# Two lightweight-convolution channel layouts for the first product of an MLP: three 64-row chunks with copies between partition halves, or one 128-row chunk and one 64-row chunk held twice

## The chip, the cores and the metric

The kernel runs on one core of a Trainium2 chip. The metric is the device time of one execution in microseconds; smaller is better. The engines have short names throughout: PE is the matrix engine (PEld its weight loads), DVE the vector engine, ACT the scalar engine, POOL the general one, SP the engine that here only issues DMAs.

## What is computed

The input x is 8 sequences of 4096 tokens with 192 channels. A causal convolution of 7 taps runs along the tokens; each of 8 groups of 24 channels has its own taps, a softmax over a small weight array. Its result goes through two products with an activation between them, all in 32-bit floats:

```python
idx = np.arange(S)[:, None] + np.arange(K)[None, :]
x_unf = x_pad[:, idx, :].reshape(B, S, K, H, group)
out = np.einsum('hk,bskhg->bshg', w, x_unf)          # 8 x 4096 x 192, K = 7, H = 8
...
h = x @ w_in                                         # 32768 x 192 times 192 x 2048
g = h * (1.0 / (1.0 + np.exp(-1.702 * h)))
return (g @ w_out).astype(np.float32)                # 2048 x 192
```

## The kernel before

**Steps.** The work is cut into 32 steps ("big") of 1024 tokens: 512 tokens of one sequence (index n = 0) and the same 512 of another (n = 1), each in two halves of 256 (index o). The tiles hold channels, or hidden features, on the partitions and tokens along the free dimension. The first step also rounds the weights and is written out by itself (`first_step`); the others are a call of `hidden` and a call of `second`.

**Layout of x.** The 192 channels are three chunks (c) of 64. Partitions 0-63 hold the tokens of o = 0, partitions 64-127 those of o = 1. `load_x` (line 126) brings x in with 8 DMAs in runs of 160 channels, `transpose_x` (145) turns 32x32 blocks on DVE, and the convolution adds seven scaled copies (`tap`, `add_taps`: on ACT, POOL, DVE and by DMAs that add). The result is `own`.

**Three multiplications.** A 32-bit product is made of three faster ones of rounded parts. `split_high` (167, ACT), `split_low` (170, DVE) and `split_both` (173, DVE) make the parts xh, xl and xd of `own`. Each needs all tokens on both partition halves, since half h of the partitions works on hidden features of its own: `cross` (178) copies each half's blocks to the other half, two DMAs on SP for each part and step.

**hidden** (245) makes the 2048 x 1024 hidden values in 16 units. A unit (j, n) is two blocks of 128 features, one per partition half, by the 512 tokens of one n, in two PSUM slots. A unit's work on PE is three passes of six matmuls of 64 rows x 512 columns, in pairs that run side by side on the two row halves of the array:

```python
upper(slot, j, n)     # wh with xh, then wl with xl (line 212, matmul in line 218)
scale(slot, engines)  # both slots times UP, in place, on ACT ("a") or DVE ("v") (line 232)
lower(slot, q, n)     # ring weights with xd, added to the scaled slots (line 223, matmul in line 227)
gelu(slot, j, n)      # ACT writes g (line 236)
```

In turn i of the loop come `upper` and `scale` of unit i, then `lower` and `gelu` of unit i-1, then `extra(i)`: transposes of a later x, parts of the convolution, and from turn 10 on sums of blocks of g for the second product (EARLY_G, DVE). Four pairs of slots take turns. The weights of `lower` come from DRAM through a ring of three buffers, each serving two units, so six units ahead; the loads are issued on SP behind the stores of the last step and the loads of x.

**second** (657 and after) makes the output with a scheme that needs fewer products than the plain one but many sums. g has four rows (r) of four blocks (j = 2n + o), each of four feature blocks: `block(r, j)`, named as a spot with number 5 + 4r + j. Unit (j, n) fills features 2j and 2j + 1 for one n. The order of everything is written out by hand in PLAN: "main" and "side" name products (32-column matmuls, four side by side, line 557), "go" issues one group of four, "sum" is a DVE sum of spots (line 620), "acc" a DMA that adds (line 625), "seed" a copy on ACT (671), "join" a sum of results, "tap" the next piece of a later convolution (513), "high", "low", "both" the splits and crossings of the next step's x, "next" the `upper` of the next step's unit 0. PLAN begins

```python
("side", 13, 16, "k0"), ("main", 1, 5, "p2", 1), ("go", 1), ("high",), ("go", 3),
("sum", 14, 14, "-", 18), ("low",), ("main", 16, 10, "p3", 0), ("go", 4), ("both",),
("main", 0, 14, "p0", 1), ("go", 1), ...
```

The engines take their instructions in this order, each its own.

Of the kernel before, what the change touches and what calls it, by code (L numbers as in the profile page):

```python
# [16 lines left out]
def kernel(  # L17
# [26 lines left out]
    NU = 2  # L44
    NV = 2
    NJ = T // Q + 1
    XT = NJ * Q
    XW = D - Q
    n3 = NC * Q
    assert B % 2 == 0 and NC == 3 and D == NC * R and HD == 3 * Q and S % TOK == 0  # L50
    assert F == 2 * NU * 2 * NV * P and PAD <= Q
# [26 lines left out]
    PAIRS = [(0, 0), (1, 1), (1, 0), (0, 1)]  # L78
    NG = 4
    assert len(PAIRS) * 4 == NF == NG * NG  # L80
# [35 lines left out]

    xt = consts.tile([P, NC, 2, XT], F32)
    own = consts.tile([P, 2 * NC, T], F32)
    xh, xl, xd = (consts.tile([P, 4 * NC, T], F32R, name=f"x{i}") for i in "hld")
    OVER = 2 * NC  # L120

    def xin_of(big):
        flat = flat_room if big == 2 else flat_g(NG - 1)
        return flat[:, 0 : 2 * NJ * XW].rearrange("p (n j d) -> p n j d", n=2, j=NJ)

    def load_x(big, ns=range(2)):

        p, c = divmod(big, CHUNKS)
        xin = xin_of(big)
        if c == 0 and 0 in ns:  # L130
            (nc.gpsimd if big else vec).memset(xin[0:R, :, 0, :], 0.0)
        for n in ns:
            for o in range(2):
                j = 1 if c == 0 and o == 0 else 0
                t = c * TOK + o * T + (j - 1) * Q
                for v in range(2):
                    q0 = o * R + v * Q
                    nc.sync.dma_start(
                        out=xin[q0 : q0 + Q, n, j:NJ, :],
                        in_=x_v[n, p, t : t + (NJ - j) * Q, v * Q : v * Q + XW].rearrange(  # L140
                            "(j i) d -> i j d", i=Q
                        ),
                    )

    def transpose_x(big, c, n=None):
        ns = slice(0, 2) if n is None else slice(n, n + 1)
        vec.transpose(
            xt[:, c, ns, :].rearrange("p n (j t) -> p (n j) t", t=Q),
            xin_of(big)[:, ns, :, :].rearrange("p n j d -> p (n j) d")[:, :, c * R : c * R + Q],
        )  # L150

    def conv_src(c, k, ns=slice(0, 2)):
        return xt[:, c, ns, Q - PAD + k : Q - PAD + k + T]

    def own_of(c, ns=slice(0, 2)):
        return own[:, 2 * c + ns.start : 2 * c + ns.stop, :]

    def conv(c, k, ns=slice(0, 2), times=vec.tensor_scalar_mul):
        src, dst, tap = conv_src(c, k, ns), own_of(c, ns), cw[:, c, k : k + 1]
        if k == 0:  # L160
            times(dst, src, tap)
        else:
            vec.scalar_tensor_tensor(
                out=dst, in0=src, scalar=tap, in1=dst, op0=ALU.mult, op1=ALU.add
            )
# [16 lines left out]
    OWN_ALL, OVER_ALL = slice(0, OVER), slice(OVER, 2 * OVER)  # L182


    wh, wl = (consts.tile([P, 2 * NU, NV, NC, P], F32R, name=f"w{i}") for i in "hl")
    RING = 3
    ring = consts.tile([P, RING, NC, P], F32R)
    N_W = NV * len(PAIRS)
    wd_dram = dram.tile([N_W, P, NC * P], F32)

    def piece_of(j):

        pi, v = j % len(PAIRS), j // len(PAIRS)
        m, u = PAIRS[pi]
        return 2 * u + m, v

    def ring_slot(q):
        return ring[:, q % RING]

    def load_ring(q):  # L200
        if q < N_W * N_BIG:
            nc.sync.dma_start(out=wide(ring_slot(q)).rearrange("p k f -> p (k f)"), in_=wd_dram[q % N_W])

    NX = 2 * N_W

    def operand(t, h, b):
        both = t[halves[h], b : b + OVER + 1 : OVER, :]
        return both if h == 0 else both[:, ::-1, :]

    KS = (1, 2, 0)  # L210

    def upper(slot, j, n):

        i, v = piece_of(j)
        for w, t in ((wh, xh), (wl, xl)):
            for k in KS:
                for h in range(2):
                    nc.tensor.matmul(  # L218
                        slot[h], w[halves[h], i, v, k, :], operand(t, h, 2 * k + n),
                        start=w is wh and k == KS[0], stop=False, skip_group_check=True,  # L220
                    )

    def lower(slot, q, n):

        for k in KS:
            for h in range(2):
                nc.tensor.matmul(  # L227
                    slot[h], ring_slot(q)[halves[h], k, :], operand(xd, h, 2 * k + n),
                    start=False, stop=k == KS[-1], skip_group_check=True,
                )  # L230

    def scale(slot, engines):
        for h in range(2):
            (act.mul if engines[h] == "a" else vec.tensor_scalar_mul)(slot[h], slot[h], UP)  # L234

    def gelu(slot, j, n):
        r = 2 * (j % len(PAIRS) + j // len(PAIRS) * len(PAIRS))
        for h in range(2):
            act.activation(  # L239
                g[:, r // NG, n, :, r % NG + h, :],  # L240
                slot[h].rearrange("p (o t) -> p o t", o=2),
                AF.Gelu_apprx_sigmoid,
            )
# [17 lines left out]
    def load_later(q):  # L261
        if q >= N_W:
            load_ring(q)
# [42 lines left out]
    def end_forms():  # L306
# [6 lines left out]
    PART = NC * P  # L313
    PIECE = CW * D
    assert PIECE == 2 * PART
    raw = [flat_g(2)[:, 2 * PART * i : 2 * PART * (i + 1)] for i in range(5)]
    raw += [osbs[:, 2 * PART * i : 2 * PART * (i + 1)] for i in range(2)]
    flat_own = own.rearrange("p b t -> p (b t)")
    raw += [flat_own[:, 2 * T : 2 * T + 2 * PART]]
    raw_out = [flat_room[:, 2 * PIECE * i : 2 * PIECE * (i + 1)] for i in range(3)] + [osbs[:, 0 : 2 * PIECE]]  # L320
    assert 10 * PART <= 4 * BLK and 6 * PIECE <= 5 * BLK
    words_in = [flat_form[:, 2 * PART * i : 2 * PART * (i + 1)] for i in range(4)]
    words_out = [flat_form[:, 8 * PART + 2 * PIECE * i : 8 * PART + 2 * PIECE * (i + 1)] for i in range(2)]
    assert 8 * PART + 4 * PIECE <= FORMS * NG * HD
    diag = flat_room[:, 4 * PIECE : 4 * PIECE + 2 * K * R].rearrange("p (c k q) -> p c k q", c=2, k=K)
    all_sel = osbs[:, 2 * PIECE : 2 * PIECE + NC * P].rearrange("i (c q) -> i c q", c=NC)
    sel = all_sel[0:H]
    ident = osbs[:, 2 * PIECE + NC * P :]
    assert 2 * PIECE + (NC + 1) * P == 4 * TOK
    fold = flat_own[:, 6 * T - R : 6 * T]  # L330
    assert 2 * PART + R <= 4 * T
# [10 lines left out]
    load_x(0, (0,))  # L342

    w_in_v = moe_w_in.bitcast(U32).rearrange(
        "(k q) (m u h v f) -> u m h v q k f", q=R, m=2, u=NU, h=2, v=NV
    )
    w_out_v = moe_w_out.bitcast(U32).rearrange("(c p) d -> p c d", p=P)

    def load_w_in(j):
        i, v = piece_of(j)  # L350
        for h in range(2):
            nc.sync.dma_start(
                out=raw[j][halves[h], :].bitcast(U32).rearrange("p (k f) -> p k f", k=NC),
                in_=w_in_v[i // 2, i % 2, h, v],
            )
# [13 lines left out]
    for c in range(NC):  # L369
        part = sel[:, c, :].rearrange("i (h q) -> i h q", h=2)  # L370
        for sign in (1, -1):
# [5 lines left out]
                base=R * c if sign == 1 else group - 1 - R * c,  # L377
                pattern=[[0, 2], [sign, R]],
                channel_multiplier=-sign * group,
            )  # L380
    nc.gpsimd.tensor_add(fold, ident[:, 0:R], ident[:, R:P])
# [12 lines left out]
    def in_part(j):  # L394
        return raw[j], words_in[j % 4]
# [35 lines left out]
    def round_w_in(j):  # L431
# [5 lines left out]
        i, v = piece_of(j)  # L437
        flat = [t[:, i, v].rearrange("p k f -> p (k f)") for t in (wh, wl)]
        low = ring_slot(j).rearrange("p k f -> p (k f)")
# [3 lines left out]
        vec.scalar_tensor_tensor(  # L443
            out=low, in0=rest, scalar=C, in1=wide(flat[0]), op0=ALU.mult, op1=ALU.subtract
        )
        nc.sync.dma_start(out=wd_dram[j], in_=wide(low))

    def round_w_out(i):
        piece = out_piece(i)
        join(piece)  # L450
        pi = PAIRS.index(divmod(i, NU))
        dsts = []
        for m in range(2):
            for v in range(2):
                for h in range(2):
                    dsts.append(
                        (
# [463 lines left out]
```

## Time and profile before

| | |
|---|---|
| median of 3 runs | 2508.43 us (2508.32 to 2519.02) |
| the profiled execution, its own time | 2508.66 us |
| its span, first to last instruction | 2506.8 us |
| busy: PE, DVE, ACT, POOL | 2288.4, 1813.8, 1587.6, 715.4 us |
| granted PE clock, mean over the span | 0.978 |
| first step (hidden from 24.58, second from 91.38) | until 144.53 us |
| second step | until 245.28 us |
| the 29 like steps | until 2428.68 us |
| last step | until the end |

Busy times of different engines lie beside each other, so they don't add up to the span. A row of the profile names the engine, the line of the kernel, the operation, what is written and read (out<-in), the shapes and the count; rows of waits name who waited for whom. In a timeline the first number is the start in us from the beginning of the span and the second the length; a bracket gives the idle time before it and what ended it.

### The profile page before, as it was taken

How to read it: one execution, taken by the hardware profiler on the slowest of the kernel's cores; microseconds unless marked ns; L12 is line 12 of the kernel's file. 1: busy time of each engine (PE TensorE's matmuls, PEld its weight loads, DVE VectorE, ACT ScalarE, POOL GpSimd, SP SyncE). 2: the span in 40 equal slices, each digit the busy share in tenths (PEclk: the TensorE clock that was granted, in tenths of full speed). 3: DMA queues.
4: the chain of work that ended last, by engine and by line, in shares of the span. 5: the costliest groups of instructions: out<-in, count | busy, mean ns of one | idle time of the engine just before them, and what ended most of it. 6: DMA issues, size and time to landing. Idle time of an engine off the chain costs nothing. (4 is left out here: it accounts for less than half of the span.)

```text
span 2506.8 us, 68873 instructions
## 1 busy us (share of the span) xinstructions
PE 2288.4 (91%) x29078; PEld 1579.1 (63%) x29078; DVE 1813.8 (72%) x2598; ACT 1587.6 (63%) x3131; POOL 715.4 (29%) x719
## 2 busy tenths in 40 slices
PE   5769999999999999999999999999999999999998
PEld 4436666666666666666666666666666666666665
DVE  4738777768777678777768777768777768777677
ACT  5636666666666666666666666666666666666643
POOL 0022323332333331333331333332333331323300
PEclk7889999999999999999999999999999999999999
DMA  7377767877766887667887777887666887667753
GB/s 185 76 140 148 153 143 143 172 162 145 150 145 141 167 175 148 147 144 144 173 168 145 150 145 145 174 168 145 147 144 141 174 171 144 145 143 144 146 119 72
DMA packets 302820, 371.69 MB, mean 148 GB/s; under 512 B 120624, under 2 KB 237104, under 8 KB 302512
## 3 DMA queue, kind: packets, MB, share of 16 engines
q0 software_dynamic: 63216, 162.49, 36.2%
q1 hardware_dynamic: 234768, 202.04, 34.2%
q8 instruction: 229, 3.75, 0.6%
q10 hardware_dynamic: 4528, 2.76, 0.5%
q14 instruction: 79, 0.65, 0.1%
HBM read 102.50 MB, written 26.74 MB: 52 GB/s over the span
## 5 line engine op out<-in xcount | busy, mean ns | idle before, releaser
L557 PE MATMUL slot<-g,w_form 128*32 128x256 f32 x8928 | 930.0, 383 | 7.0 <-DVE room L620 4.2
L239 ACT ACTIVATE g<-slot 128x512 f32<-128x512 f32 x1024 | 551.9, 597 | 275.2 <-PE slot L227 246.7
L227 PE MATMUL slot<-xd,ring 64*128 64x512 f32 x3072 | 561.1, 405 | 136.7 <-DVE slot L234 74.5
L234 DVE TENSOR_SCALAR slot<-slot 128x512 f32<-128x512 f32 x651 | 432.0, 694 | 332.3 <-PE slot L218 328.7
L557 PEld LDWEIGHTS slot<-g,w_form 128*32 128x32 f32 x8928 | 478.2, 111 | 161.1 <-DVE room L620 13.5
L557 PE MATMUL slot<-g,w_out_s 128*32 128x256 f32 (+1 forms) x6336 | 532.1, 404 | 38.9 <-DVE g L620 29.1
L218 PE MATMUL slot<-xh,wh 64*128 64x512 f32 x3072 | 513.3, 393 | 21.9 <-ACT wh L440 17.1
L620 DVE TENSOR_TENSOR g<-g 128x1024 f32<-128x1024 f32 x403 | 483.4, 1218 | 61.7 <-DMA g<-room 41.3
L227 PEld LDWEIGHTS slot<-xd,ring 64*128 64x128 f32 x3072 | 359.9, 186 | 242.6 <-DVE slot L234 134.9
L218 PE MATMUL slot<-xl,wl 64*128 64x512 f32 x3072 | 507.7, 389 | 4.5 <-DMA xl<-xl 3.4
L668 ACT COPY room<-slot 32x256 f32<-32x256 f32 x651 | 237.4, 365 | 306.2 <-PE slot L557 300.2
L557 PEld LDWEIGHTS slot<-g,w_out_s 128*32 128x32 f32 x6336 | 262.1, 112 | 266.0 <-issue 51.2
L218 PEld LDWEIGHTS slot<-xh,wh 64*128 64x128 f32 x3072 | 357.2, 185 | 83.6 <-ACT wh L440 20.8
L218 PEld LDWEIGHTS slot<-xl,wl 64*128 64x128 f32 x3072 | 360.7, 185 | 55.0 <-issue 4.8
L513 ACT ACTIVATE g<-xt,cw 128x512 f32<-128x512 f32 x406 | 288.1, 723 | 132.8 <-POOL own L530 72.6
L625 POOL DMA_DIRECT2D g<-g x124 | 128.5, 1036 | 564.9 <-PE slot L557 544.4
L234 ACT ACTIVATE slot<-slot 128x512 f32<-128x512 f32 x373 | 210.0, 579 | 113.4 <-PE slot L218 113.4
L557 PE MATMUL slot<-osbs,w_form 128*32 128x256 f32 x2232 | 226.3, 379 | 0.5 <-issue 0.4
L530 POOL TENSOR_TENSOR own<-own,g 128x512 f32<-128x512 f32 x174 | 220.0, 1284 | 4.5
L557 PE MATMUL slot<-room,w_form 128*32 128x256 f32 x2232 | 171.4, 379 | 0.0
L625 POOL DMA_DIRECT2D g<-osbs x31 | 27.1, 874 | 415.4 <-ACT g L239 415.4
L557 PEld LDWEIGHTS slot<-osbs,w_form 128*32 128x32 f32 x2232 | 116.2, 110 | 43.1 <-issue 1.3
(102 smaller groups left out, 1846.9 us busy)
## 6 DMA issues: line engine op xcount, KB each, us to landing
g<-g POOLq DMA_DIRECT2D x124, 512.0 KB, 13.6
ring<-wd_dram SPq DMA_DIRECT2D x251, 192.0 KB, 2.4
g<-in_x_dram SPq DMA_DIRECT2D x232, 180.0 KB, 4.1
xh<-xh SPq DMA_DIRECT2D x62, 384.0 KB, 3.7
xl<-xl SPq DMA_DIRECT2D x62, 384.0 KB, 6.9
xd<-xd SPq DMA_DIRECT2D x62, 384.0 KB, 12.1
out_dram<-osbs SPq DMA_DIRECT2D x186, 128.0 KB, 4.3
g<-osbs POOLq DMA_DIRECT2D x31, 512.0 KB, 5.0
```

The source lines that it names most:

```text
L218: nc.tensor.matmul(slot[h], w[halves[h], i, v, k, :], operand(t, h, 2 * k + n), start=w is wh and k == KS[0], stop=False, skip_group_check ...
L227: nc.tensor.matmul(slot[h], ring_slot(q)[halves[h], k, :], operand(xd, h, 2 * k + n), start=False, stop=k == KS[-1], skip_group_check=True,)
L234: (act.mul if engines[h] == "a" else vec.tensor_scalar_mul)(slot[h], slot[h], UP)
L239: act.activation(g[:, r // NG, n, :, r % NG + h, :], slot[h].rearrange("p (o t) -> p o t", o=2), AF.Gelu_apprx_sigmoid,)
L513: act.mul(home, conv_src(c, k), cw[:, c, k : k + 1])
L530: eng.tensor_add(dst, dst, home)
L557: nc.tensor.matmul(dst, w, t, start=first, stop=last, skip_group_check=True)
L620: (vec.tensor_add if op == "+" else vec.tensor_sub)(v(dst), v(a), v(b))
L625: nc.gpsimd.dma_start(out=spot(dst), in_=spot(a), accum_op=ALU.add)
L668: act.copy(to, d)
```

## The change

The channels are laid out in another way. Channels 0-127 lie on all 128 partitions, for every token of n = 0 (a = 0) and of n = 1 (a = 1). Channels 128-191 lie on both halves, o = 0 on partitions 0-63 and o = 1 on 64-127 (a = 2), and their weights are held twice, once for each half. So each half needs only its own tokens, and `cross` goes. x is loaded in runs of 32 channels with 16 DMAs a step.

A unit is now one block of 128 features by all 1024 tokens: a slot per o, with n = 0 and 1 side by side in it. A pass is two matmuls of 128 rows, one per slot, and a pair of 64 rows, one per slot; from pass to pass their order alternates (`phase`). `lower` and `gelu` of a unit come two turns after its `upper` instead of one, between the two passes of `upper`; those of the last unit (`end`) have moved into PLAN, behind the fourth group. The ring has six buffers, one unit each. The engines of `scale` are dealt out anew. In the first step the weights are rounded in pieces a third larger, two of the operations go from DVE to POOL, and the first convolution is made with 128-row matmuls.

```diff
+    def load_x(big, parts=(0, 2, 1)):
+        ...
+        for a in parts:
+            if a < 2:
+                ...
+                for q in range(4):
+                    load(one[q * Q : (q + 1) * Q, a], a, c * TOK - Q, q * Q, int(c == 0))
+            else:
+                ...
+                for n in range(2):
+                    for q in range(4):
+                        o, v = divmod(q, 2)
+                        load(two[q * Q : (q + 1) * Q, n], n, c * TOK + o * T - Q, P + v * Q, int(c == 0 and o == 0))
...
-    def cross(t, to, of, eng=nc.sync):
-        for o in range(2):
-            eng.dma_start(out=wide(t[halves[1 - o], to, :]), in_=wide(t[halves[o], of, :]))
...
-    def upper(slot, j, n):
-        i, v = piece_of(j)
-        for w, t in ((wh, xh), (wl, xl)):
-            for k in KS:
-                for h in range(2):
-                    nc.tensor.matmul(
-                        slot[h], w[halves[h], i, v, k, :], operand(t, h, 2 * k + n),
-                        start=w is wh and k == KS[0], stop=False, skip_group_check=True,
-                    )
...
+    def pass_of(slot, w, t, first=False, last=False):
+        phase[0] += 1
+        for step in range(2):
+            if (step + phase[0]) % 2:
+                for o in range(2):
+                    nc.tensor.matmul(
+                        slot[o], w[:, 0, :], t[:, o : o + 3 : 2, :],
+                        start=first and step == 0, stop=last and step == 1, skip_group_check=True,
+                    )
+            else:
+                for o in range(2):
+                    nc.tensor.matmul(
+                        slot[o], w[halves[o], 1, :], t[halves[o], 4:6, :],
+                        start=first and step == 0, stop=last and step == 1, skip_group_check=True,
+                    )
...
+    def end_unit(big, tiles, r):
+        q = big * NF + r
+        lower(tiles[r % 4], q)
+        gelu(tiles[r % 4], r)
+        if q + RING >= NF:
+            load_ring(q + RING)
...
-        for i in range(NX + 1):
-            if i < NX:
-                if i or not begun:
-                    upper(tiles[i % 4], *divmod(i, 2))
-                scale(tiles[i % 4], scales[i])
-            if i:
-                j, n = divmod(i - 1, 2)
-                q = big * N_W + j
-                lower(tiles[(i - 1) % 4], q, n)
-                gelu(tiles[(i - 1) % 4], j, n)
-                if n == 1:
-                    load_later(q + RING)
+        for i in range(NF):
+            if i or not begun:
+                upper_high(tiles[i % 4], i)
+            if i > 1:
+                end_unit(big, tiles, i - 2)
+            if i or not begun:
+                upper_low(tiles[i % 4], i)
+            scale(tiles[i % 4], scales[i])
             extra(i)
+        end_unit(big, tiles, NF - 2)
...
-        vec.tensor_sub(rest, w, wide(flat[0]))
+        nc.gpsimd.tensor_sub(rest, w, wide(flat[0]))
         act.mul(flat[1], rest, C)
-        vec.scalar_tensor_tensor(
-            out=low, in0=rest, scalar=C, in1=wide(flat[0]), op0=ALU.mult, op1=ALU.subtract
-        )
+        nc.gpsimd.tensor_sub(low, wide(flat[1]), wide(flat[0]))
...
-        ("side", 13, 16, "k0"), ("main", 1, 5, "p2", 1), ("go", 1), ("high",), ("go", 3),
+        ("side", 13, 16, "k0"), ("main", 1, 5, "p2", 1), ("go", 1), ("high",), ("go", 3), ("end",),
...
         def high():
             if more:
-                split_high(own, 0, OVER)
-                cross(xh, OVER_ALL, OWN_ALL)
+                split_high(own, 0, 6)
...
-        hidden(0, tiles, ["aa"] * NX, extra, begun=False)
+        hidden(0, tiles, ["av", "vv"] * (NF // 2), extra, begun=False)
+        end_unit(0, tiles, NF - 1)
...
-    SCALES = ["aa", "aa", "va", "vv"] + ["va", "vv"] * 6
+    SCALES = ["av", "av", "av", "vv"] + ["av", "vv"] * 6
```

More of the change, by code (lines that the diff above doesn't have):

```diff
@@ L114, in kept @@
         return spot(KEPT_LATE)[0:n3, i % NG, :]
[L117 to L120, printed above, removed]
+    turned = [consts.tile([P, 2, n * Q], F32, name=f"xt{i}") for i, n in enumerate((NJ2, NJ))]
+    own = consts.tile([P, 6, T], F32)
+    flat_own = own.rearrange("p b t -> p (b t)")
+    xh, xl, xd = (consts.tile([P, 6, T], F32R, name=f"x{i}") for i in "hld")
@@ L160, in conv, with tap_of, own_of @@
+    def tap_of(a, k):
+        return cw[:, a // 2, k : k + 1]
+    def own_of(a):
+        return own[:, 2 * a : 2 * a + 2, :]
+    def conv(a, k, times=vec.tensor_scalar_mul):
+        src, dst, tap = conv_src(a, k), own_of(a), tap_of(a, k)
         if k == 0:
@@ L223, in lower @@
[L223 to L238, printed above, removed]
+    wh, wl = (consts.tile([P, NF, 2, P], F32R, name=f"w{i}") for i in "hl")
@@ L239, in gelu, with upper_high, upper_low, lower @@
+    def upper_high(slot, r):
+        pass_of(slot, wh[:, r], xh, first=True)
+    def upper_low(slot, r):
+        pass_of(slot, wl[:, r], xl)
+    def lower(slot, q):
+        pass_of(slot, ring[:, q % RING], xd, last=True)
+    def scale(slot, engines):
+        for o in range(2):
+            (act.mul if engines[o] == "a" else vec.tensor_scalar_mul)(slot[o], slot[o], UP)
+    def gelu(slot, r):
+        for o in range(2):
             act.activation(
-                g[:, r // NG, n, :, r % NG + h, :],
@@ L341 @@
     act.activation(early, ident[0:H, 0:1], AF.Exp)
[L342 to L346, printed above, removed]
+    load_x(0, (0, 2))
+    w_in_v = moe_w_in.bitcast(U32)
     w_out_v = moe_w_out.bitcast(U32).rearrange("(c p) d -> p c d", p=P)
     def load_w_in(j):
-        i, v = piece_of(j)
-        for h in range(2):
+        dst = raw[j].bitcast(U32).rearrange("p (r k f) -> p r k f", r=2, k=2)
+        cols = slice(4 * P * j, 4 * P * (j + 1))
+        for on, k, rows in ((slice(0, P), 0, 0), (halves[0], 1, P), (halves[1], 1, P)):
+            n = on.stop - on.start
             nc.sync.dma_start(
-                out=raw[j][halves[h], :].bitcast(U32).rearrange("p (k f) -> p k f", k=NC),
-                in_=w_in_v[i // 2, i % 2, h, v],
+                out=dst[on, :, k, :], in_=w_in_v[rows : rows + n, cols].rearrange("q (r f) -> q r f", r=2)
             )
@@ L368 @@
     nc.gpsimd.memset(sel, 1.0)
-    for c in range(NC):
+    for c in range(2):
         part = sel[:, c, :].rearrange("i (h q) -> i h q", h=2)
@@ L478 @@
     warm(5)
-    for c in range(NC):
+    for c in range(2):
         nc.tensor.matmul(
@@ L629, with second @@
     SIDE_HALF = (0, 0, 1, 0, 1, 0, 1)
-    def second(big, bx, bs, by, more, next_first):
+    def second(big, bx, bs, by, more, end, next_first):
         mains, sides = (bs[0], bx[0], by[0]), (bx[1], bs[1], by[1])
@@ L702, in second @@
             join=lambda d, a, op, b: add_up(value, d, a, op, b), turn=out_turn, store=out_store,
-            tap=next_tap, high=high, low=low, both=both, next=next_first,
+            tap=next_tap, end=end, high=high, low=low, both=both, next=next_first,
         )
@@ L707, in second, with first_conv @@
         assert not side and not now["steps"] and count[0] == NC * len(SIDE_HALF)
[L709 removed]
+    def first_conv(a):
         for k in range(K):
[L711 to L727 removed]
@@ L748, in high_first, with first_src @@
-    def high_first(n, i):
-        src, b = first_blocks(n)[i]
-        split_high(src.unsqueeze(1), b, b + 1)
-        cross_first(xh, n, KS[i])
-    def first_step(tiles):
-        one, two = slice(0, 1), slice(1, 2)
-        make_diag()
-        transpose_x(0, 1, 0)
-        transpose_x(0, 2, 0)
+            nc.tensor.matmul(
+                pairs[1][a], diag[:, k, :], conv_src(a, k), start=(k == 0), stop=(k == K - 1), skip_group_check=True
+            )
+    def first_src(a):
+        return (own_of(2) if a == 2 else pairs[1][a].rearrange("p (o t) -> p o t", o=2)), 2 * a, 2 * a + 2
@@ L784, in first_step @@
+        for k in range(2, K):
+            conv(2, k)
+        split_low(*first_src(0))
+        split_both(*first_src(0))
+        split_high(*first_src(2))
+        round_w_in(0)
+        split_high(*first_src(1))
+        split_low(*first_src(2))
+        split_low(*first_src(1))
+        split_both(*first_src(2))
+        split_both(*first_src(1))
         split(in_part(1))
@@ L842, in first_step @@
         turns = second_plain(pb, pa, pc, at)
-        for q in range(N_W, N_W + RING):
-            load_ring(q)
-        upper(pf, 0, 0)
+        upper_high(pf, 0)
+        upper_low(pf, 0)
         for m, n, src in turns:
@@ L888 @@
             ready.extend((c, k) for c in (1, 0, 2) for k in range(K))
-        second(big, pb, pa, pc, more, (lambda: upper(pf, 0, 0)) if more else lambda: None)
+        begin = lambda: (upper_high(pf, 0), upper_low(pf, 0))
+        second(big, pb, pa, pc, more, end, begin if more else lambda: None)
         tiles = [pf, pa, pb, pc]
```

252 lines of the change are left out of this document (89 added, 163 removed).

## The prediction

> **What bounds the kernel now.** First the page's span, then the windows, which cut the run into stages:
>
> ```profile
> span 2506.8 us, 68873 instructions
> ```
>
> ```profile
> 24.58:91.38 66.80, 47.69 (x288) 30.24 (x288) 36.53 (x82) 49.44 (x98) 0.00 (x0) 0.83 0.49 139
> 144.53:210.15 65.62, 39.97 (x289) 31.17 (x289) 40.41 (x54) 28.76 (x53) 6.10 (x7) 0.81 0.47 92
> 245.28:2428.68 2183.40, 2038.76 (x26452) 1417.95 (x26448) 1615.97 (x2259) 1421.32 (x2795) 677.29 (x663) 0.99 0.74 152
> 1148.20:1186.88 38.68, 35.09 (x292) 28.68 (x289) 27.80 (x38) 24.11 (x46) 13.49 (x12) 1.00 0.57 122
> 1186.88:1222.51 35.63, 34.43 (x626) 20.19 (x626) 27.93 (x41) 25.30 (x52) 10.44 (x12) 1.00 0.97 192
> ```
>
> Columns: length, then busy PE, PEld, DVE, ACT, POOL, granted clock, DMA share, GB/s. From 245.28 to 2428.68 the same step runs 29 times, 2183.40 / 29 = 75.3 us each. I work on one of them: a hidden stage H of 38.68 (lines 218 and 227) and an output stage S of 35.63 (line 557). PE is busy 2038.76 of the 2183.40, more than any other: nearly without a gap in S, with gaps in H. The waits of PE say which:
>
> ```profile
> PE slot L227 <- DVE slot L234: 74.5, 66, 6.3
> PE slot L227 <- ACT slot L234: 38.7, 32, 1.6
> PE slot L557 <- DVE g L620: 29.3, 24, 3.2
> ...
> PE slot L218 <- DMA xh<-xh: 4.8, 3, 3.6
> ```
>
> (total, times, longest.) The copies between the halves, which the change removes, cost PE 4.8 us for xh in the whole run, and less for xl, which stands further down, and xd: they are hidden. The gaps of H are the third multiplication (line 227) waiting for the scaling of its slot (line 234).
>
> **The price of PE's work in H.** PE's timeline around the start of H and late in S (start, length, what, count; neighbours of one kind are merged), then its weight loads:
>
> ```profile
> 1147.87 0.39 PE L557 MATMUL slot<-g,w_out_s 128*32 128x256 f32 x3
> 1147.89 0.38 PE L557 MATMUL slot<-g,w_form 128*32 128x256 f32 x1
> 1148.20 0.96 PE L218 MATMUL slot<-xh,wh 64*128 64x512 f32 x6
> 1149.00 0.86 PE L218 MATMUL slot<-xl,wl 64*128 64x512 f32 x6
> ...
> 1153.10 0.90 PE L227 MATMUL slot<-xd,ring 64*128 64x512 f32 x6
> 1153.78 0.90 PE L218 MATMUL slot<-xh,wh 64*128 64x512 f32 x6
> ...
> 1217.02 3.83 PE L557 MATMUL slot<-g,w_form 128*32 128x256 f32 x65
> ```
>
> ```profile
> 1148.20 0.53 PEld L218 LDWEIGHTS slot<-xh,wh 64*128 64x128 f32 x6 [0.41 <-issue]
> ...
> 1185.99 0.53 PEld L227 LDWEIGHTS slot<-xd,ring 64*128 64x128 f32 x5 [0.41 <-DVE slot L234]
> 1186.88 0.12 PEld L557 LDWEIGHTS slot<-g,w_out_s 128*32 128x32 f32 x3 [0.36 <-issue]
> ```
>
> One pass (six matmuls of 64x512, three pairs side by side) takes 1153.78 - 1153.10 = 0.68, 0.227 a pair; 48 passes are 32.6 of H's 38.68. In S four matmuls run side by side; 16 such groups and one matmul take 3.83, so a group takes (3.83 - 0.38) / 16 = 0.216.
>
> After, a pass is two matmuls on all 128 rows, one behind the other, and one pair on 64 rows: again three times 512 columns. The trace shows no 128-row matmul of 512 columns. Six loads hide under a pass now (0.53 of 0.68), so four will. Bounds: three times 0.216 or three times 0.227, 0.65 to 0.68; I take **0.65**, since 0.227 is seen where every pair takes a new weight in both halves, and the full-row matmuls come in twos with the same one.
>
> New is that each pass goes once from 128-row to 64-row matmuls or back (the order alternates, so there is none between passes): 48 **switches** per step, where the kernel has two now. The two price it. Into H: a next group would have started at 1147.87 + 0.216 = 1148.09; line 218 starts at 1148.20, 0.11 late, and the first pass takes 0.80 instead of 0.68, 0.12 more. The loader's row shows why: idle for 0.41 for no reason but issue, its first load starting with the matmul; nothing was loaded ahead. Together 0.23. Out of H: five matmuls from 1185.99 should hand over after three pairs, at 1186.67; line 557 starts at 1186.88, 0.21 late, 0.12 of it a first load of the same kind inside the pass. That leaves 0.09 for the change itself, and going back to 128 columns the load of 0.12 comes on top. Ends for a switch between 128x128 and 64x128: nothing, if rows alone don't count, and 0.23. I take **0.22**: both shown changes, in either direction, stop the loader.
>
> The Trainium skill ("TensorEngine Tiling (Array Packing)", Key Properties) says that changing the tiling mode, not just the tile, drains the engine, and lists 128x128 and 64x128 as separate modes. By that rule all 48 count. The trace agrees on its two kinds of change; none in it changes rows alone.
>
> So a pass costs 0.65 + 0.22 = 0.87.
>
> **The waits in H.** DVE and ACT in the same step:
>
> ```profile
> 1171.25 0.70 DVE L234 TENSOR_SCALAR slot<-slot 128x512 f32<-128x512 f32 x1
> ...
> 1184.65 1.29 DVE L234 TENSOR_SCALAR slot<-slot 128x512 f32<-128x512 f32 x2
> 1185.85 2.35 DVE L620 TENSOR_TENSOR g<-g 128x1024 f32<-128x1024 f32 x2
> ```
>
> ```profile
> 1159.60 0.72 ACT L513 ACTIVATE g<-xt,cw 128x512 f32<-128x512 f32 x1 [2.50 <-POOL own L530]
> ...
> 1186.77 1.08 ACT L239 ACTIVATE g<-slot 128x512 f32<-128x512 f32 x2 [2.05 <-PE slot L227]
> 1187.74 1.49 ACT L168 ACTIVATE xh<-own 128x1536 fp32r<-128x1536 f32 x1
> 1189.25 0.37 ACT L668 COPY room<-slot 32x256 f32<-32x256 f32 x1
> ```
>
> From the scaling of unit 10 (done 1171.25 + 0.70) to that of unit 15 (done 1184.65 + 1.29) DVE works 14.0 us nearly without a pause, with sums of line 620 between; PE needs less and waits. The order of these stays, and the count too ("va" only becomes "av"; units 0 and 1 go from "aa" to "av"). The third multiplication one unit later gives PE more to do meanwhile: from the end of unit 10's low pass to unit 15's third come 16 passes and four groups of S, 16 x 0.87 + 0.86 = 14.8, against DVE's 0.6 + 14.0 = 14.6. The wait for DVE **goes**, barely. The wait for ACT (38.7) goes as well: the tap at 1159.60 is held by POOL until 11.4 us into H; the gelu of unit 2, now queued behind it on ACT, is done some 13 in, and its slot is wanted after 16 passes, 14.1 in.
>
> What is late next is in S. The first sum there, spot 14 minus spot 18, reads block 1 of row 3. Now units with even number fill that block, and unit 14 is the last: DVE does the sum in the row of 1185.85, which starts before unit 15's gelu (1186.77). After the change every unit fills all four blocks of its row, so the sum needs the gelu of **unit 15**, which stands in ACT behind unit 14's gelu, the 1.49 of xh and a copy of 0.37. With T the end of unit 14's third pass, which ends H: gelu 14 to T + 1.0, xh to T + 2.5, copy to T + 2.8, gelu 15 to T + 3.9, sum (1.2) to T + 5.1. PE is at its user, the ninth group of S, at T + 0.86 (four groups) + 0.22 + 0.87 (unit 15) + 0.1 + 0.86 = T + 2.9: it waits 2.1 us. Behind the sum DVE holds the low and both splits and the next sums; they come 2.6 us later after T than now, PE 3.3 later, so no more waits come of it.
>
> **The other edits.** Rows of SP, of the DMA issues, of ACT's scalings, and of DVE in the second step:
>
> ```profile
> 1147.72 6.85 SPq L554 DMA_DIRECT2D out_dram<-osbs  x6
> 1154.69 4.02 SPq L138 DMA_DIRECT2D g<-in_x_dram  x8
> ```
>
> ```profile
> ring<-wd_dram SPq DMA_DIRECT2D x251, 192.0 KB, 2.4
> g<-in_x_dram SPq DMA_DIRECT2D x232, 180.0 KB, 4.1
> ```
>
> ```profile
> L234 ACT ACTIVATE slot<-slot 128x512 f32<-128x512 f32 x373 | 210.0, 579 | 113.4 <-PE slot L218 113.4
> ```
>
> ```profile
> 162.74 13.89 DVE L163 SCALAR_TENSOR_TENSOR own<-xt,cw,own 128x512 f32<-128x512 f32 x18
> ```
>
> x comes in 16 DMAs instead of 8, in runs of 128 bytes instead of 640. SP ends the stores at 1154.57, 6.4 into H, and issues x for 8.0 us instead of 4.0, so the ring load for unit 6 goes out some 15 into H and lands by 17.5, the last x by 18.5. They are wanted at 20 (unit 6's third pass, after 23 passes) and 22: hidden; without the slow passes the ring load could be 0.5 late. Ring loads grow by a third in bytes and are fetched six units ahead, as now. Transposes, taps and splits keep their number and size. Without the copies the adding DMAs of S have more room; what PE waits for sums in S is 29.3 in all, so this is worth between 0 and 29; I take 0, with the smaller packets and bigger ring on the other side. Two more switches around unit 15 in S: 0.22 + 0.1. First step: ACT is busy 49.44 of its 66.80 and loses 24 of 32 scalings (0.58 each, 14), while the rounding of weights grows by a third and two subtractions per piece go to POOL: between 0 and -14, I take -6. Second step (65.62): DVE's convolutions end at 176.6 as before, and now every unit has a scaling on DVE behind them; 43 passes are left from 177.2, which makes 214.6 against 210.15: +4.5.
>
> **Sum.** H: 48 x 0.87 + 0.22 + 0.32 = 42.3, +3.6; S +2.1; 5.7 a step. 29 steps 165; the second step +4.5 + 2.4 = 7; the last one, without xh on ACT, +5; the first -6. 171 on the profiled 2506.8 and the 1.9 around it (2508.66; the median of the runs is 2508.43): **2680**. Its own range, with the pass from 0.65 to 0.68, the switch 0.19 to 0.23 and the DMA's 29: 2640 to 2725.
>
> **Rivals.**
>
> *Rows alone don't stop the loader* (0.17). For it: no change of rows alone is in the trace. Against: both changes that are. Pass 0.65. Then PE outruns the others: unit 6's slot waits 1.9 for ACT's tap and gelu, DVE's tail 16 x 0.65 + 0.86 = 11.3 against 14.6 makes 3.3, the new sum still 1.3 (T + 5.7 against T + 4.4). 48 x 0.65 + 0.5 + 1.9 + 3.3 + 1.3 = 38.2 against 38.68: -0.5 a step, **2489**. This is the faster side; it decides below about 0.04 us per switch.
>
> *Drain, but loads ahead* (0.13). Pass 0.75. DVE's tail 1.7, the slot 0.5, the sum 1.2: 36.0 + 0.5 + 3.4 = 39.9, +1.2 a step, **2544**. The Trainium skill ("TensorE: Matmul & The Clock Gate", Part 2) lets the engine pull weight loads ahead of running matmuls into a background buffer; by that this rival would hold. Within a mode the trace agrees (loads hide under the 0.227 pairs), at 1148.20 it doesn't (idle 0.41).
>
> *Switches cost, but the new wait is taken up* (0.08): waits that S has anyway shrink by it. 2680 - 31 x 2.1 = **2615**.
>
> *It doesn't do what it says for the time*: the copies go, but are worth only the few us of waits above; this is contained in each case.
>
> **Chances.** Forecast 0.58, rivals as given, 0.04 for others. The range 2485 to 2725 leaves out half of the fast rival and the upper edge. About 0.5% (2496 to 2521) is what a measurement of this kernel can tell from no change: faster 0.14, same 0.08, slower 0.78.
>
> **What would show it.** The starts of successive matmuls in a pass of H: 0.216 apart within a mode, some 0.43 where the rows change, and the loader idle there; passes 0.87 apart. PE's waits for line 234 nearly gone; a wait of 2 us in S for the sum behind the gelu of unit 15. Wrong would be passes of 0.65 with growing waits for DVE, or no wait in S.

## The result and the profile after

The changed kernel takes 2591.65 us (median of four, 2590.59 to 2592.49) against 2508.38 for the kernel before: ratio 1.0324, 95% interval 1.0294 to 1.0354. It is slower, as forecast, but by 83 us where 171 were forecast. Its profiled execution took 2591.83, with this span:

```profile
span 2589.9 us, 63267 instructions
...
PE 2526.6 (98%) x25920; PEld 1395.9 (54%) x25920; DVE 1861.0 (72%) x2631; ACT 1569.4 (61%) x3034; POOL 745.9 (29%) x738
```

PE's own work grew from 2288.4 to 2526.6 and now fills the span. I cut both traces where PE's matmuls change from one stage to the other and took means over the 29 like steps. H counts unit 15's third pass (1.10) also where it stands inside S.

| us | before | after | change | forecast |
|---|---|---|---|---|
| first step | 144.53 | 131.97 | -12.6 | -6 |
| second step | 100.75 | 106.49 | +5.7 | +7 |
| a like step | 75.29 | 78.20 | +2.91 (x29 = 84.4) | +5.7 (165) |
| of it H | 38.93 | 43.56 | +4.63 | +3.6 |
| of it S | 36.36 | 34.65 | -1.71 | +2.1 |
| last step | 78.13 | 83.58 | +5.5 | +5 |

The miss lies in S, which became shorter instead of longer; H missed by 1.0 the other way, so the two misses partly cancel. One step of the changed kernel in the windows (columns as in the prediction):

```profile
1098.71:1140.93 42.22, 42.22 (x189) 22.84 (x188) 27.44 (x38) 22.67 (x41) 12.62 (x10) 1.00 0.44 96
1140.93:1176.67 35.74, 35.26 (x631) 20.49 (x629) 29.59 (x43) 26.48 (x54) 11.53 (x16) 1.00 0.74 136
```

In H PE has no idle time left: busy 42.22 of 42.22, against 35.09 of 38.68 before. In S the DMA share fell from 0.97 to 0.74. The waits of PE in the whole run:

```profile
PE slot L544 <- DVE g L607: 14.8, 31, 0.5
PE slot L221 <- ACT slot L237: 12.3, 1, 12.3
PE slot L221 <- DVE slot L237: 11.9, 1, 11.9
```

The waits for the scaling, 113 us before, are down to one of 12.3 and one of 11.9 outside the like steps. The new wait is there, 31 times, once a step: at most 0.5 us, not 2.1. PE's timeline in H, and then the weight loads:

```profile
1101.16 0.51 PE L221 MATMUL slot<-xh,wh 64*128 64x512 f32 x2
1101.50 0.40 PE L221 MATMUL slot<-xl,wl 64*128 64x512 f32 x2
1101.83 0.73 PE L215 MATMUL slot<-xl,wl 128*128 128x512 f32 x2
1102.39 0.62 PE L215 MATMUL slot<-xh,wh 128*128 128x512 f32 x2
1102.95 0.50 PE L221 MATMUL slot<-xh,wh 64*128 64x512 f32 x2
```

```profile
1101.16 0.19 PEld L221 LDWEIGHTS slot<-xh,wh 64*128 64x128 f32 x2 [0.36 <-issue]
1101.27 0.19 PEld L221 LDWEIGHTS slot<-xl,wl 64*128 64x128 f32 x2
1101.83 0.30 PEld L215 LDWEIGHTS slot<-xl,wl 128*128 128x128 f32 x2 [0.37 <-issue]
```

From 1101.16 to 1102.95 lie two passes and two switches: 0.895 a pass, against a forecast of 0.87. At each switch the loader is idle for 0.36, for no reason but issue, and its first load starts with the matmul that needs it: rows alone stop it, as forecast. The single starts of this H stage show how a switch is paid. Within a mode they lie 0.227 to 0.237 apart; over a change of rows 0.326, and the second start behind it 0.338. Together that is 0.20 to 0.21 late.

### The profile page after: what moved, and what is told of

Read it like the earlier page. It is cut to its first block, busy times and chain, and to the rows that moved or that the text cites. A ratio compares the mean times of both kernels' runs of the same rounds, so it can differ in the third digit from the quotient of the medians.

```text
span 2589.9 us, 63267 instructions
## 1 busy us (share of the span) xinstructions
PE 2526.6 (98%) x25920; PEld 1395.9 (54%) x25920; DVE 1861.0 (72%) x2631; ACT 1569.4 (61%) x3034; POOL 745.9 (29%) x738
## 4 chain that ended last, share of the span: by engine, by line
PE 89%; ACT 5%; DVE 4%; DMA 1%; issue 1%; POOL 0%; SPq 0%; DVEq 0%; POOLq 0%
PE slot L544 37%; PE slot L215 33%; PE slot L221 19%; ACT g L241 3%; ACT xh L183 2%; DVE g L607 1%; DVE own L178 1%; DMA w_form<-w_form 1%; ACT room L655 0%; POOL w_form L306 0%; SPq L135 0%; DVE w_form L411 0%; DVE w_form L408 0%; DVE w_form L419 0%; ACT wh L437 0%
## 5 line engine op out<-in xcount | busy, mean ns | idle before, releaser
L237 DVE TENSOR_SCALAR slot<-slot 128x512 f32<-128x512 f32 x737 | 491.3, 694 | 483.0 <-PE slot L215 242.3
L215 PE MATMUL slot<-xh,wh 128*128 128x512 f32 x1024 | 352.2, 425 | 11.2 <-ACT wh L437 7.5
L215 PE MATMUL slot<-xl,wl 128*128 128x512 f32 x1024 | 356.6, 429 | 0.0
L215 PE MATMUL slot<-xd,ring 128*128 128x512 f32 x1024 | 351.8, 425 | 0.4 <-ACT slot L237 0.4
L221 PE MATMUL slot<-xd,ring 64*128 64x512 f32 x1024 | 234.7, 454 | 24.2 <-ACT slot L237 12.3
L215 PEld LDWEIGHTS slot<-xh,wh 128*128 128x128 f32 x1024 | 172.9, 189 | 134.1 <-issue 95.6
L215 PEld LDWEIGHTS slot<-xl,wl 128*128 128x128 f32 x1024 | 170.9, 189 | 129.0 <-issue 106.2
L215 PEld LDWEIGHTS slot<-xd,ring 128*128 128x128 f32 x1024 | 173.4, 189 | 115.2 <-issue 90.9
L221 PE MATMUL slot<-xh,wh 64*128 64x512 f32 x1024 | 234.1, 454 | 0.0
L221 PE MATMUL slot<-xl,wl 64*128 64x512 f32 x1024 | 227.7, 441 | 0.0
```

The lines of the kernel that those rows point to most:

```text
L215: nc.tensor.matmul(slot[o], w[:, 0, :], t[:, o : o + 3 : 2, :], start=first and step == 0, stop=last and step == 1, skip_group_check=True,)
L221: nc.tensor.matmul(slot[o], w[halves[o], 1, :], t[halves[o], 4:6, :], start=first and step == 0, stop=last and step == 1, skip_group_check ...
L237: (act.mul if engines[o] == "a" else vec.tensor_scalar_mul)(slot[o], slot[o], UP)
```

## The experiments

My theory after the result: the switches cost what was forecast; the late third multiplication takes the waits of H away; and the copies, costed at nothing, were worth about 60 us, because they slowed the DMAs that add, on which S depends. The rival for S: its gain comes from the new layout itself (smaller packets, other sums), and the copies were hidden, as I had read the waits.

**Copies put back into the changed kernel.**

```diff
+    other = consts.tile([P, 6, T], F32)
+
+    def cross(t):
+        for o in range(2):
+            nc.sync.dma_start(out=other[halves[1 - o], :, :], in_=wide(t[halves[o], :, :]))
...
+                cross(xh)
...
+                cross(xl)
...
+                cross(xd)
```

> The changed kernel with the six copies between the halves issued again at their old places, into a tile that nobody reads. Theory A (the output stage S got shorter because the adding DMAs have the DMA engines to themselves): S goes from 34.6 us back towards 36, the time from 2592 to 2620 to 2635. Rival B (S got shorter because the hidden stage no longer ends in a stall, with DVE late and the clock at half): no change, 2587 to 2597.

Measured: 2654.28, ratio to the kernel before 1.0565 (1.0536 to 1.0594), 62.6 above the changed kernel: the copies cost even more than the range says, so rival B can't be the whole account (what of it holds is in the next experiment). H is 43.60 as without them, S 36.71 instead of 34.65. How long the adding DMAs need from issue to landing, in the changed kernel and then with the copies (count, KB each, median us):

```profile
g<-g POOLq DMA_DIRECT2D x124, 512.0 KB, 7.8
```

```profile
g<-g POOLq DMA_DIRECT2D x124, 512.0 KB, 13.5
...
other<-xh SPq DMA_DIRECT2D x60, 384.0 KB, 5.0
```

Nobody reads the copies, yet PE waits for them at one remove:

```profile
PE slot L549 <- DMA g<-g: 24.7, 31, 2.0
PE slot L549 <- DVE g L612: 19.5, 39, 1.2
```

The first wait isn't in the changed kernel at all. In the kernel before the same DMAs took 13.6:

```profile
g<-g POOLq DMA_DIRECT2D x124, 512.0 KB, 13.6
```

**Copies taken out of the kernel before.** The body of `cross` is empty; the parts are set to zero once at the start.

```diff
-        for o in range(2):
-            eng.dma_start(out=wide(t[halves[1 - o], to, :]), in_=wide(t[halves[o], of, :]))
+        pass
+
+    for part in (xh, xl, xd):
+        nc.gpsimd.memset(wide(part), 0.0)
```

> The kernel before without its copies between the halves: the parts that they would fill hold zeros, set once, so the output lacks what those blocks would add. Theory A: S falls from 36.4 to some 35.2 us, the time from 2508 to some 2470. Rival B: S stays, 2500 to 2510, since the copies cost PE only 4.8 and 3.4 us of waits.

Measured: 2435.94, ratio 0.9697 (0.9675 to 0.9719), 72 us below. A like step falls from 75.29 to 73.46: S from 36.36 to 34.66, H only from 38.93 to 38.80. The adding DMAs land in 7.2. Of the 72 us, 53 lie in the like steps; 19 lie in the first two steps and are not taken apart.

S has the length that it has after the change (34.65), but not in the same way. Here PE has no idle time in S and loses time at its start instead, as the kernel before does too. A window of the kernel before around the start of S at 1262.46, with a granted clock (third from the right) of 0.52:

```profile
1262.40:1264.20 1.80, 1.80 (x21) 0.84 (x24) 0.69 (x1) 1.80 (x3) 0.00 (x0) 0.52 0.30 73
```

Over the first 2.5 us of S the granted clock is 0.50 to 0.68 in 10 of the 29 like steps of the kernel before and 0.52 to 0.65 in 15 of them without copies. In such a step the first eleven groups of S, 0.216 apart elsewhere, come 1.4 to 1.7 us late together; in the mean of all 29 that is 0.49 and 0.87. In the changed kernel the clock there is 1.00 in every step. With this taken off, S falls from 35.87 to 33.79 without copies, 2.08, which is what putting them back cost (2.06). So the copies are most of S's gain, and the lowered clock, which rival B of the first experiment named, is 0.49 of it. The new wait, which the changed kernel's S contains, takes a part back.

**Copies put back where the adding DMAs aren't.** As the first experiment, but issued in turns 7, 8 and 9 of the hidden stage.

```diff
+            if i in (7, 8, 9) and big + 1 < N_BIG:
+                cross((xh, xl, xd)[i - 7])
```

> The changed kernel with the six copies put back once more (into a tile that nobody reads), but issued in turns 7, 8 and 9 of the hidden stage instead of in the output stage. Theory (the copies cost because they delay the DMAs that add, and the sums and matmuls of the output stage behind them): the adding DMAs of 512 KB land in about 8 us as in the changed kernel, the output stage keeps its 34.65, and the time is 2590 to 2605, near the 2591.65 without copies. Rival (the bytes or their issue on SP cost wherever they stand): 2630 to 2655, as with the copies in the output stage (2654.28).

Measured: 2588.8 (2586.95 to 2589.84), ratio 1.0302 (1.0286 to 1.0317): the same bytes on the same queue cost nothing here.

```profile
g<-g POOLq DMA_DIRECT2D x124, 512.0 KB, 7.8
...
other<-xh SPq DMA_DIRECT2D x60, 384.0 KB, 3.9
```

S keeps 34.64. So it isn't the bytes or the issue on SP, it is that they meet the adding DMAs in S. This is a probe and no remedy: real copies of xh, xl and xd are needed when H begins.

**The late third multiplication alone**, in the kernel before, with unit 15's end in PLAN as in the change:

```diff
-            if i:
-                j, n = divmod(i - 1, 2)
...
+            if i or not begun:
+                upper_high(tiles[i % 4], *divmod(i, 2))
+            if i > 1:
+                end_unit(big, tiles, i - 2)
+            if i or not begun:
+                upper_low(tiles[i % 4], *divmod(i, 2))
```

> The kernel before with one part of the change alone: the third multiplication one unit later, that of the last unit behind the fourth group of S, as in the changed kernel; layout and copies stay. Theory: PE's waits for the scaling (113 us in all) shrink, to DVE's tail of 14.6 against 12.7 and a wait of up to 1.9 for unit 6's slot: 2 us less a step, 2508 to 2430 to 2460. Rival: the waits only move to the slots and into S: 2495 to 2515.

Measured: 2468.02 (2456.86 to 2479.83), ratio 0.9826 (0.9784 to 0.9868), a gain of about 40 us, somewhat less than expected, and less sure in size than the others, since its runs lie 23 us apart; the profiled one is the fastest of them. The wait for the scaling is down to 18.5 us in all (16.6 for DVE, 1.9 for ACT), but a part comes back in front of the slots:

```profile
PE slot L216 <- ACT g L247: 42.6, 29, 1.5
...
PE slot L235 <- DVE slot L242: 16.6, 34, 5.4
```

H falls from 38.93 to 37.94 only: without the switches PE runs ahead and waits for the gelu that frees its slot (29 times, about once a step). S falls from 36.36 to 35.71. Its clock is 1.00 at the start of all 29 like S stages: with the late third multiplication alone the lowered clock is gone, with the copies and the layout as before. Why the stall at the end of H, which is there in every step before, lowers the clock in only some of them was not tried.

**Twice the switches.** Every pass begins with the 128-row matmuls, so the rows change within each pass and again between passes.

```diff
-            if (step + phase[0]) % 2:
+            if step == 0:
```

> The changed kernel with the 128-row matmuls first in every pass, so the rows change twice a pass, 96 times a step instead of 48. Theory (0.21 us for each change, in either direction): 48 x 0.21 = 10 us more a step, 2592 to 2880 to 2920. Rival (what a pass has over 0.68 comes from the 128-row matmuls): below 2650.

Measured: 2920.18, ratio 1.1626 (1.1606 to 1.1645). PE's timeline, and the hidden stage of a like step:

```profile
1101.74 0.73 PE L215 MATMUL slot<-xl,wl 128*128 128x512 f32 x2
1102.40 0.49 PE L221 MATMUL slot<-xl,wl 64*128 64x512 f32 x2
1102.83 0.73 PE L215 MATMUL slot<-xh,wh 128*128 128x512 f32 x2
```

```profile
1262.64:1313.71 51.07, 51.07 (x189) 22.72 (x188) 29.31 (x39) 22.88 (x41) 12.64 (x10) 1.00 0.37 79
```

A pass takes 1102.83 - 1101.74 = 1.09, 0.195 more than 0.895, for one switch more; by the windows, 51.07 - 42.22 over 47 passes is 0.19. The price is linear: a pass of three streams of 0.23 with one switch or with two. Only 29 x 8.70 = 252 of the 328 us come from the like steps; the expected 10 us a step would be 290, and that the time met the upper end of the expectation is luck. Most of the rest is in the first two steps (68 us), which the expectation left out and where the granted clock (third from the right) is lower; here a window of the first, of this kernel and then of the changed one:

```profile
60.00:100.00 40.00, 40.00 (x86) 16.84 (x86) 18.83 (x33) 18.75 (x32) 9.77 (x8) 0.50 0.07 24
```

```profile
60.00:100.00 40.00, 34.21 (x171) 15.74 (x175) 32.13 (x52) 24.67 (x40) 7.71 (x6) 0.87 0.32 81
```

**No rows to change.** The second part of each pass also with 128-row matmuls, two of them instead of a pair.

```diff
-                        slot[o], w[halves[o], 1, :], t[halves[o], 4:6, :],
+                        slot[o], w[:, 1, :], t[:, 4:6, :],
```

> The changed kernel with 128-row matmuls in place of the 64-row pairs too: channels 128-191 of both halves are added up, so the output is another one; PE's operands keep their size. No change of rows is left in the hidden stage, and a pass is four matmuls one behind the other. Theory: 4 x 0.23 = 0.92 against 0.90 now: 2595 to 2630. Rival (128-row matmuls are the slow ones): over 2750.

Measured: 2598.1, ratio 1.0345 (1.0324 to 1.0366), 6.5 above the changed kernel.

```profile
1101.64 0.62 PE L215 MATMUL slot<-xh,wh 128*128 128x512 f32 x2
1102.09 0.62 PE L221 MATMUL slot<-xh,wh 128*128 128x512 f32 x2
1102.54 0.61 PE L221 MATMUL slot<-xl,wl 128*128 128x512 f32 x2
```

Four 128-row streams take 0.90 a pass, 0.227 each in the mean of the like steps. So the pair that runs side by side saves a stream of 0.23 and pays 0.20 of it back at the switch.

**The split of xh behind unit 15's end**, to shorten the new wait:

```diff
-        ... ("go", 1), ("high",), ("go", 3), ("end",),
+        ... ("go", 4), ("end",), ("high",),
```

> The changed kernel with xh of the next step made behind the last unit's gelu instead of ahead of it. Theory (the prediction's new wait in S, measured 0.48 us a step, stands behind xh's 1.5 us on ACT): the wait goes, 2592 to 2574 to 2580. Rival (it only moves to the splits and the sums behind them): 2586 to 2596.

Measured: 2587.33, ratio 1.03 (1.0282 to 1.0317), 4 us less; the wait falls from 0.48 to 0.34 a step. The rival was nearer. The trace of the changed kernel shows why: ACT, then DVE, then PE (T is 1140.93 here).

```profile
1141.04 1.09 ACT L241 ACTIVATE g<-slot 128x512 f32<-128x512 f32 x2 [0.71 <-PE slot L221]
1142.01 1.49 ACT L183 ACTIVATE xh<-own 128x1536 fp32r<-128x1536 f32 x1
1143.53 0.37 ACT L655 COPY room<-slot 32x256 f32<-32x256 f32 x1
1143.92 1.09 ACT L241 ACTIVATE g<-slot 128x512 f32<-128x512 f32 x2
```

```profile
1145.03 1.23 DVE L607 TENSOR_TENSOR g<-g 128x1024 f32<-128x1024 f32 x1 [2.17 <-ACT g L241]
```

```profile
1142.80 0.50 PE L221 MATMUL slot<-xd,ring 64*128 64x512 f32 x2
1143.23 0.73 PE L215 MATMUL slot<-xd,ring 128*128 128x512 f32 x2
1143.90 1.93 PE L544 MATMUL slot<-g,w_form 128*32 128x256 f32 x32
1146.31 0.42 PE L544 MATMUL slot<-g,w_out_s 128*32 128x256 f32 x3 [0.48 <-DVE g L607]
```

ACT is free again at 1143.90, the moment at which PE goes on from unit 15's third pass: xh held up very little, and without it ahead the wait is 0.14 shorter.

**Passes of a turn grouped.** The three passes of a turn are issued together: first all their 128-row matmuls, then all their pairs, or the other way in the next turn. The hidden stage shown below has 17 switches; the changed kernel has 47.

```diff
+            for slot, w, t, first, last in jobs if step == 0 else sorted(jobs, key=lambda job: not job[4]):
                 for o in range(2):
...
+        passes_of(upper_high + lower_of(tiles[r % 4], q) + upper_low)
```

> The changed kernel, with the three passes of a turn made together: the 128-row matmuls of all three, then the 64-row pairs of all three (next turn the other way round), so one change of rows a turn instead of three, 16 to 18 a step instead of 48. Theory: each change costs 0.21 us, so PE has 6.5 us less to do in a step; DVE's tail (14.6 against 14.0) gives 0 to 1.5 back: the step falls from 78.2 to 72 to 74 us, the time to 2390 to 2460. Rival (the 128-row matmuls or their loads are slow, not the change of rows): 2580 to 2600.

Measured: 2447.75 (2446.49 to 2448.28), ratio 0.9744 (0.9722 to 0.9766): faster than both kernels.

```profile
1051.33 0.62 PE L217 MATMUL slot<-xl,wl 128*128 128x512 f32 x2
1051.78 0.61 PE L217 MATMUL slot<-xh,wh 128*128 128x512 f32 x2
...
1053.23 0.50 PE L217 MATMUL slot<-xd,ring 64*128 64x512 f32 x2
1053.57 0.40 PE L217 MATMUL slot<-xh,wh 64*128 64x512 f32 x2
1053.80 0.40 PE L217 MATMUL slot<-xl,wl 64*128 64x512 f32 x2
```

Starts of 0.23 run on until the one change of rows. H falls from 43.56 to 38.96, S stays (34.50). 30 switches less at 0.20 would be 6.0 a step, and 4.6 came. Of the 1.4 that are missing, 0.8 lie in one place: in the mean of the like steps, three starts from unit 6's first pass on come 0.54, 0.49 and 0.49 behind the one before instead of 0.23. There PE's loads wait for the gelu that frees unit 6's slot and then for a scaling; on ACT both stand behind a tap that POOL holds up. This is the wait for unit 6's slot that the prediction's first rival counted with 1.9. The other 0.6 are single late starts that are not taken apart. The same kernel with xh behind unit 15's end:

> The grouped kernel (2447.75) with the split of xh behind the gelu of unit 15 instead of ahead of it. It took 4 us from the changed kernel. If the wait it shortens is on the path here as well, 2441 to 2446; if what is left of the wait is set by another sum or DMA, 2446 to 2450.

Measured: 2447.81, ratio 0.9741 (0.9725 to 0.9758): no difference.

**Grouped over two turns**, which leaves 10 switches in a hidden stage instead of 17; the third passes of the two turns' units stand among the new ones of both.

```diff
+        for i in range(0, NF, 2):
...
+                if new:
+                    first += new[0] + old + new[1]
+                    second += old + new[0] + new[1]
+            passes_of(first, second)
```

> The grouped kernel, but with the passes of two turns made together, so one change of rows every two turns: some 8 a step fewer. Theory (each costs 0.21 us of PE, and PE is what bounds the hidden stage): 1.7 us less a step if nothing waits, 0.5 less if DVE's tail takes it back: 2448 to 2390 to 2435. Rival (with 16 changes left DVE's tail already bounds the stage): 2440 to 2465.

Measured: 2667.14, ratio 1.0617 (1.0598 to 1.0636), a clear miss. Waits and timeline of PE, then ACT:

```profile
PE slot L217 <- ACT slot L233: 140.2, 139, 10.9
PE slot L217 <- DVE slot L233: 27.1, 32, 11.9
```

```profile
1011.55 0.73 PE L217 MATMUL slot<-xh,wh 64*128 64x512 f32 x2
1013.26 0.50 PE L217 MATMUL slot<-xd,ring 64*128 64x512 f32 x2 [0.98 <-ACT slot L233]
...
1014.89 1.09 PE L217 MATMUL slot<-xd,ring 64*128 64x512 f32 x2 [0.65 <-DVE slot L233]
```

```profile
1010.65 2.07 ACT L237 ACTIVATE g<-slot 128x512 f32<-128x512 f32 x4 [3.16 <-PE slot L217]
1012.58 0.63 ACT L233 ACTIVATE slot<-slot 128x512 f32<-128x512 f32 x1
```

The scaling (line 233) is back on the path. The two units of a block end close together, so the gelus of two units (2.07 on ACT) stand ahead of ACT's scaling, and the next block wants the first scaled slot behind only two of its own matmuls (those at 1011.55). What the order saves in switches it loses in distance between a unit's second and third pass.

## Why the prediction was right in direction and wrong in size

- **The pass and the switch.** Right. A switch was taken at 0.22; doubling it gives 0.19 to 0.20, the single starts 0.20 to 0.21. The stream was a little under: 0.65 a pass taken, some 0.69 shown, since a 128-row matmul with a load of its own starts 0.227 to 0.237 after the last and not 0.216. 48 passes of 0.895 to 0.903 instead of 0.87 are 1.2 to 1.6 us more, of which 1.0 shows in H's change, since its edges took less than the 0.54 put on them and H before is 38.93 in the mean, not 38.68. The prediction says that the trace shows no 128-row matmul of 512 columns. It does: 384 in the first step (128*32 128x512), but with 32 columns of weights, and they start 0.43 apart in fours, so they wouldn't have given the price of the rounded ones. Since a change of rows alone costs 0.2 and the loader is idle for 0.36 at it, the rivals of 2489 and 2544 fell.
  The Trainium skill ("TensorEngine Tiling (Array Packing)", Key Properties) says that a change of tiling mode drains the engine; the runs agree that a change of rows alone costs time, 0.19 to 0.21 each. The Trainium skill ("TensorE: Matmul & The Clock Gate", Part 2) says that weight loads are pulled ahead of running matmuls if the row groups don't conflict or the load goes to a background buffer; the trace agrees within a mode, where matmuls with a load each start 0.227 to 0.237 apart, and across this change no load was ahead.
- **The waits of H.** Right: they went, and PE fills H. The late third multiplication alone shows that they go without the switches too, though a part comes back as a wait for slots.
- **The new wait in S.** Right in place and mechanism, wrong in size: 0.48 of idle time where 2.1 was taken; by the starts of the matmuls, 0.67. The step that failed is "T + 0.86 (four groups)". From T, 1140.93, to unit 15's pass at 1142.80 it is 1.86: a "go" is eight of the trace's matmuls, two groups of four. This stands twice in the sum, so PE is at the sum's user 4.9 behind T and not 2.9, while the sum ends at T + 5.3 (forecast T + 5.1). The same slip stands in DVE's tail, where it only strengthens the conclusion.
- **The copies.** Wrong: "this is worth between 0 and 29; I take 0". The bound was what PE waits for sums in S (29.3). It was no bound: most of the gain isn't in rows of waits. What the runs showed in its place is 2.06 to 2.08 us a step, some 60 us in all. In S, idle time fell by 0.85 a step (1.33 to 0.48) with a new wait of 0.48 in it, and the stage by 1.71; in the changed kernel the copies bring 1.31 of idle time and 2.06 of length. Stalls shorter than the modelled overlap of a matmul (0.38 long, 0.216 apart) don't appear as idle. The rows that could have warned were the landing of the adding DMAs, 13.6, and the DMA share of 0.97 in S.
- **The clock at the start of S.** Not in the prediction: the step it worked on has 1.00 there. In the mean of the like steps the lowered clock cost the kernel before 0.49 a step, and with the late third multiplication it is gone.
- **First, second and last step.** -12.6 for -6, near the far end of the bound; +5.7 and +5.5 for +7 and +5.
- **The rivals.** "The new wait is taken up" gave 2615 and comes nearest in time, though not for its reason: the wait wasn't absorbed, it was small. That the copies are worth "only the few us of waits" fell.

Per step the miss of 2.8 closes to 0.2: H +1.0, the wait -1.4 (0.67 for 2.1), the copies -2.1 by the first experiment, the clock at the start of S -0.5, together -3.0. What takes the last 0.2 back is open.

## What to carry to other kernels

Count how often the rows of successive matmuls change before packing a short contraction: on this kernel a change costs nearly the stream that the packing saves. Packing with a switch in every pass was worth 6.5 us against four full streams, ordering the packed matmuls by rows another 144. Cost a DMA by what runs at the same time, not by who waits for it: the same copies cost 62 us beside the adding DMAs and nothing in the hidden stage. Before a wait is priced, read off the trace how many instructions one item of a hand-written order issues.

## What was not expected of the hardware

- A change of rows delays two matmuls, not one: the first starts 0.326 after its predecessor and the second 0.338, against 0.23.
- Copies of 384 KB that nobody reads lengthen the landing of adding DMAs of 512 KB from 7.8 to 13.5 us.
- With twice the switches, PE's granted clock was 0.50 from 60 to 100 us, where the changed kernel has 0.87; in the like steps shown it is 1.00 in both. What lowers it was not tried.
- In the kernel before, the granted clock at the start of S is 0.50 to 0.68 in 10 of 29 like steps and 1.00 in the others, although PE stalls at the end of H in all of them; with the late third multiplication it is 1.00 in all 29.
